# Rotary attention into a mixture of experts on one core: plan products and gathers one slot earlier, a dense step one tile later, four casts on another engine

## The chip, the cores and the metric

The kernel runs on one core of a Trainium2 chip. The metric is the device time of one execution in microseconds (us). A core has five engines that run their own instruction streams and wait for each other through semaphores: TensorE (PE in the profile, its weight loads PEld), VectorE (DVE), ScalarE (ACT), GpSimd (POOL) and SyncE (SP), which here only issues transfers. Data moves between the chip's main memory and the core's SBUF by DMA; matmul results land in PSUM.

## What is computed

The reference is attention with rotary position coding, followed by a layer of one dense network and eight experts. Shapes: batch 8, 8 heads, 576 positions, head size 64; the layer sees 4608 tokens of width 512, and all its hidden widths are 512.

```python
q_rot, k_rot = (rotate(q), rotate(k))
scores = scale * np.matmul(q_rot, k_rot.transpose(0, 1, 3, 2))
attn = softmax(scores)                      # row maximum subtracted
attn_out = np.matmul(attn, v)
x = attn_out.transpose(0, 2, 1, 3).reshape(B * S, H * D)

y_dense = np.maximum(x @ w1_dense, 0.0) @ w2_dense
logits = x @ w_gate
expert_idx = np.argmax(logits, axis=1)      # one expert per token
y_moe[mask] = gate_w[mask, None] * (np.maximum(x[mask] @ w1[e], 0.0) @ w2[e])
return y_dense + y_moe
```

## The kernel before

**Attention.** Heads are taken two at a time, so there are 32 pairs, four to a batch; `attention()` walks them with `for i in range(NP + 1)` and, inside, nine slots `t`. In slot `t` of pair `i` TensorE computes one block of scores of pair `i + 2` (`s1_block`, L369) whose row maximum VectorE takes (L371), one strip of transposed scores of pair `i` (`s2_strip`, L392) that ScalarE exponentiates into `pm` (L409), and some products with the values for pair `i - 1` (`av_part`, L431), which VectorE scales (`av_scale`, L442 to L445). The order on each engine is the order in which the Python code writes it: the schedule is written by hand, with tables that say which extra step goes to which slot `(i, t)`.

The rotary coding of pair `i + 5` runs on GpSimd as four long element-wise instructions (`stage_rope`, L314 to L317), after which a DMA transposes the result (L327) and another copies the keys to their own buffer (`stage_keys`, L355).

**The values.** The values of a batch arrive in float32 in one buffer `vf`. `cast_v(b, u)` (L273) turns the 128 columns of pair `u` of batch `b` into float16, 640 elements per partition in five groups; `v_turn` (L281, L282) transposes them on TensorE for the gate's weights. The casts of batch 0 stand ahead of the loop (pairs 0 and 1) and in slots 3 and 5 of pair 0 (pairs 2 and 3); those of batch 1 in slots 1 and 6 of pair 2 and later.

**The plan of tokens.** Tokens are sorted by expert into tiles of 128 rows. For the first six batches that plan is made while attention still runs: its steps sit in the table `steps[i, t]`. Its closing products (`e`, L633) are two runs of 15 matmuls of one-hot rows on TensorE into one PSUM tile; `f` (L638 to L653) turns the sum into row numbers on VectorE. `draw(0, u)` then gathers the rows of tile `u` of the first group (`gather`, L852, an indirect DMA that GpSimd issues, from the stored attention output `xd`) and has SyncE transpose it by DMA (`turn`, L858). For every tile but the first, ScalarE copies one column of row numbers ahead of the gather (L869).

**The experts.** `run_groups` walks the tiles `t` in groups of four. Per tile: the expert's first product (`expert_in`, L906) and its activation (L909); the transposition of that (`expert_turn`, L914); one to two of the four dense first products of the group (`dense_in`, L897, activation L899), which read the transposed tiles of the whole group at once; and the out tile of an earlier tile (`out_tile`, L921 and L923), whose rows VectorE copies (L925) and GpSimd scatters to the output (L926). How many dense products go to tile `t` is the tuple that the diff changes. A group's dense products are put on the list one tile ahead of the group's first tile.

Of the kernel before, what the change touches and what calls it, by code (L numbers as in the profile page):

```python
# [25 lines left out]
def kernel(  # L26
# [12 lines left out]
    nc = tc.nc  # L39
    B, H, S, D = q.shape  # L40
# [22 lines left out]
    VB = 2  # L63
    VC = D + 2 + 2 * E
    OA, VA, OB, WB = 2 * E, 2 * E + 2, D, D + 2
    v16s = []
    for i in range(VB):
        t = const_p.tile([P, HP, 5, 2 * VC], fp16, name=f"v16_{i}")
# [6 lines left out]
    with tc.tile_pool(name="setup", bufs=1) as setup_p:  # L75
# [37 lines left out]
        for b0, b1 in ((0, 5), (5, 9)):  # L113
            n = b1 - b0
# [14 lines left out]
    for i in range(NAT):  # L129
        t = early.tile([P, 9, 2, D], bf16, name=f"nat{i}")  # L130
# [139 lines left out]
                              v[b, a::2, MAIN:S, :].rearrange("h p d -> p h d"))  # L270

    def cast_v(b, u):
        nc.scalar.copy(v16s[b % VB][:, u, :, VA:VA + 2 * D].rearrange("p n (h d) -> p n h d", d=D),  # L273
                       vf[:, u].rearrange("p (h n) d -> p n h d", n=5))

    def v_turn(b, u):
        if u == 0:
# [393 lines left out]
    def attention():  # L671
        for f in turn_early(0):
            f()
        stage_keys(1, nc.sync)
        for part in range(2):
            stage_load(1, 0, 2, part, (0, HP))
        split_gate()
        for i in range(1, KK):
            pad_keys(i)
        for t in range(9):  # L680
            s1_block(0, t)
        for t in range(9):
            s1_block(1, t)
            if t == 1:
                shift_rows(0)
                for part in range(2):
                    stage_load(1, 2, 4, part, ())
                nc.scalar.copy(ident_h, ident_f)
                nc.scalar.preload_act_table_set("natural_log_exp_and_others")
                cast_v(0, 0)  # L690
            if t == 2:
                early_2 = turn_early(2)
            if 3 <= t < 7:
                early_2[t - 3]()
        cast_v(0, 1)
        for i in range(3, RA):
            stage_rope(i)
        stage_transpose(3)
        gt = gate_steps(0, wg)
        rk, got0 = rank_steps(0, wg, attn_sums)  # L700
        WS = [(i, 5) for i in range(5, 22, HP)] + [(24, 5), (25, 1), (25, 6), (26, 1), (26, 6)]
        assert len(WS) == E + 2
        steps = {(27, 0): gt[0:1], (22, 0): [route_first, route_ranks, route_tokens], (27, 2): gt[1:2], (27, 4): gt[2:3]}
        AVS = (((0, 0), (0, 1), (1, 3), (3, 4), (4, 5), (5, 7), (7, 8), (8, 9), (9, 10)),
               ((0, 0), (0, 1), (1, 3), (3, 4), (4, 5), (5, 6), (6, 7), (7, 8), (8, 10)))
        loads = {}
        for b in range(2, B):
            n = (b - 2) * HP
            for at, f, *x in ((n, stage_load, b, 0, 2, 0, ()), (n + 1, stage_load, b, 0, 2, 1, ()),
                              (n + 1, stage_tails, b, 0), (n + (1 if b in (2, B - 1) else 2), stage_tails, b, 1),  # L710
                              (n + 2, stage_load, b, 2, 4, 0, ()), (n + 3, stage_load, b, 2, 4, 1, ())):
                loads.setdefault(at + (1 if b == 2 else 0), []).append((f, *x))
        V0 = (0, 2), (0, 7), (1, 3), (1, 5)
        v_steps = {}
        for b in range(1, B):
            n = b * HP
            for u, (c, r) in enumerate((((n - 3, 6), (n - 3, 8)), ((n - 2, 3), (n - 2, 5)), ((n - 1, 3), (n - 1, 5)), ((n, 2), (n, 5)))):
                if b == B - 1 and u > 1:
                    c = (n - 1, 1 + 3 * (u - 2))
                if b == 1 and u < 2:  # L720
                    c, r = ((n - 2, 1), (n - 2, 5)) if u == 0 else ((n - 2, 6), (n - 2, 8))
                v_steps.setdefault(c, []).append((cast_v, b, u))
                v_steps.setdefault(r, []).append((v_turn, b, u))
        for i in range(NP + 1):
            for t in range(9):
                if i + 2 < NP:
                    s1_block(i + 2, t)
                if i < NP:
                    s2_strip(i, t)
                if 1 <= i <= NP and t >= 1:  # L730
                    for k in range(*AVS[i % HP == 1][t]):
                        av_part(i - 1, k)
                    if t == 8:
                        av_scale(i - 1)
                if i == 0 and t in (3, 5):
                    cast_v(0, 2 + t // 5)
                if (i, t) in V0:
                    v_turn(0, V0.index((i, t)))
                if i < NP and (i, t) in v_steps:
                    for f, *x in v_steps.pop((i, t)):  # L740
                        f(*x)
                if t == 1 and i + 1 < NP:
                    shift_rows(i + 1)
                if t == 2 and i + RA < NP:
                    stage_rope(i + RA)
                if t == (0 if i > 1 else 2) and i + KA < NP:
                    stage_keys(i + KA, nc.sync)
                if t == 2 and i + LA < NP:
                    stage_transpose(i + LA)
                if t == 2:  # L750
                    for f, *x in loads.pop(i, ()):
                        f(*x)
                if (i, t) in WS:
                    n = WS.index((i, t))
                    load_w(*((w1d, moe_w1_dense), (w2d, moe_w2_dense))[n] if n < 2 else (w1e[:, n - 2], moe_w1[n - 2]))
                if t == 5:

                    if i % HP == 0 and i // HP + 1 < B:
                        stage_v(i // HP + 1)
                    if i % HP == 3 and HP < i < NP - HP or i == NP - 3:  # L760
                        x_store(i // HP - 1)
                    if i == NP - RA:
                        early_cm.__exit__(None, None, None)
                        open_late()
                        wa = late["wa"]
                        pl, mm, fin = plan_steps(0, wa, attn_sums, got0)
                        w2 = [lambda e=e: load_w(late["w2e"][:, e], moe_w2[e]) for e in range(E)]
                        steps[27, 6] = rk[0:1] + [route_parts]
                        steps[27, 5] = w2[0:2]
                        steps[27, 7] = w2[2:5]  # L770
                        steps[28, 0] = rk[1:2] + w2[5:6] + pl[0:1]
                        steps[28, 2] = gt[3:4]
                        steps[28, 3] = rk[2:3] + w2[6:8] + pl[1:2]
                        steps[28, 6] = rk[3:4]
                        steps[29, 0] = pl[2:3]
                        steps[29, 3] = pl[4:6]
                        steps[29, 8] = rk[4:5]
                        steps[30, 0] = rk[5:6]
                        steps[30, 6] = mm[0:1]
                        steps[30, 7] = mm[1:] + [fin, lambda: draw(0, 0)]  # L780
                        for n in range(1, GT):
                            steps[31, 3 * n - 2] = [lambda n=n: draw(0, n)]
                        steps[31, 8] = pl[3:4]
                if (i, t) == (NP - 1, 2):
                    logit_sum(B - 2)
                for st in steps.pop((i, t), ()):
                    st()
            if i < NP:
                s2_tails(i, 0)
            if i < NP:  # L790
                s2_tails(i, 1)
            if i in (0, 1) or i < NP and i % HP == 0:
                u0, u1 = (2 * i, 2 * i + 2) if i < 2 else (0, HP)
                for u in range(u0, u1, 2):
                    v_gate(u)
                v_part(i // HP, 0, u0, u1)
                steps.setdefault((i + 1, 0), []).append(lambda b=i // HP, u0=u0, u1=u1: v_part(b, 1, u0, u1))
            if i == NP - 1:
                draw(1, 0)
        assert not steps and not v_steps and not loads  # L800
        logit_sum(B - 1)
        x_store(B - 1, nc.scalar)
# [18 lines left out]
    GT = 4  # L821
# [42 lines left out]
    def draw(g, u):  # L864
        t = g * GT + u
        if u == 0:
            room(g, late["first"], g, 1)
        if t:
            nc.scalar.copy(take_i[:, t:t + 1], tk[:, t:t + 1])  # L869
        gather(g, u)  # L870
        if g == 0:
            turn(g, u)
# [80 lines left out]
    def run_groups(gs, plan):  # L953
# [23 lines left out]
        for g in gs:  # L977
            n = sizes[g]
            for u in range(n):
# [18 lines left out]
                    turns.append(ahead.pop(0))  # L998
                if t + 1 in starts:
                    dense += dense_steps(starts[t + 1])  # L1000
                m = len(dense) if t == last else (0, 1, 1, 2, 0, 1, 2, 2)[t] if t < 2 * GT else 1
                for st in dense[:m]:
                    st()
                del dense[:m]
# [49 lines left out]
```

## Time and profile before

| | us |
|---|---|
| median of 3 runs (460.21 to 466.31) | 464.79 |
| the profiled execution | 464.98 |
| its span, from the first to the last instruction | 463.2 |
| TensorE busy | 402.8 |
| GpSimd busy | 342.2 |
| VectorE busy | 320.9 |
| ScalarE busy | 295.8 |

The profile is of one execution; the runs around it differ by up to 6 us. Rows of a timeline give the start in us, the busy time, engine, source line and operation, what is written and read, and in brackets how long the engine stood idle before the row and what it seems to have waited for. Rows of the chain that ended last give start, duration, engine, tile and line. A row with `x4` holds four instructions that follow each other. Mean granted TensorE clock over the span: 0.972 of full speed.

### The profile page before, as it was taken

Reading aid. Unit: us, or ns where it says so; the run is one execution under the profiler, and the core shown is the slowest. Engines: PE = TensorE matmul, PEld = TensorE weight load, DVE = VectorE, ACT = ScalarE, POOL = GpSimd, SP = SyncE. Lnnn points to the kernel's source line nnn. Section 1 sums busy time; section 2 is a strip of 40 time slices with the busy share of each in tenths; the row PEclk is TensorE's granted clock in tenths of the full one; section 3 lists DMA queues with packets and bytes.
Section 4 is the critical chain, followed back from the end, with each engine's and each line's share of the span. In section 5 each row is a group of like instructions: output and inputs, shape, how many; then the busy total and the mean of one; then the engine's idle time right before and its main releaser. Section 6 shows DMA issues by size and latency. Waiting matters only on the chain.

```text
span 463.2 us, 11065 instructions
## 1 busy us (share of the span) xinstructions
PE 402.8 (87%) x4091; PEld 250.0 (54%) x4108; DVE 320.9 (69%) x579; ACT 295.8 (64%) x577; POOL 342.2 (74%) x279
## 2 busy tenths in 40 slices
PE   1688898989999999999988988786989999999991
PEld 0346566656666666666666665563435444444440
DVE  7887789888899999899999899964357211212221
ACT  6598787877887887887877886683333343333320
POOL 1799989989989979989999957933546455554332
PEclk9799899998999999999999998998999999999997
DMA  6866668988768868879968989928777777787442
GB/s 173 230 173 156 137 141 232 155 157 249 152 148 243 178 164 241 155 126 279 165 176 192 177 159 219 228 53 186 164 161 172 171 189 194 184 186 196 107 120 76
DMA packets 134251, 80.65 MB, mean 174 GB/s; under 512 B 93461, under 2 KB 127765, under 8 KB 134197
## 3 DMA queue, kind: packets, MB, share of 16 engines
q1 hardware_dynamic: 119460, 55.34, 52.0%
q0 software_dynamic: 14240, 23.73, 23.9%
q10 hardware_dynamic: 496, 0.85, 0.5%
q8 instruction: 35, 0.57, 0.5%
q14 instruction: 20, 0.16, 0.1%
HBM read 52.05 MB, written 14.42 MB: 144 GB/s over the span
## 4 chain that ended last, share of the span: by engine, by line
PE 64%; DMA 11%; ACT 9%; DVE 9%; issue 3%; SPq 2%; POOL 0%; POOLq 0%; ACTq 0%; DVEq 0%
PE s L369 10%; PE s L392 9%; PE av L431 9%; PE pd L897 7%; PE py L923 7%; PE py L921 7%; PE pe L906 7%; ACT pm L409 5%; DVE negm L371 5%; DMA qT<-mT 4%; PE vps L281 2%; PE s L365 2%; PE s L389 2%; DMA vf<-in_v_dram 2%; PE mps L377 2%
## 5 line engine op out<-in xcount | busy, mean ns | idle before, releaser
L371 DVE TENSOR_REDUCE negm<-s 128x1 f32<-128x576 f32 x288 | 205.3, 749 | 21.8 <-PE s L369 20.6
L409 ACT ACTIVATE pm<-s 128x512 f16<-128x512 f32 x280 | 161.5, 598 | 43.1 <-PE s L392 39.2
L431 PEld LDWEIGHTS <-pm 128*128 128x128 f16 x1600 | 87.3, 98 | 53.8 <-issue 21.6
L369 PE MATMUL s<-kx,qT 126*128 126x288 bf16 x512 | 108.0, 294 | 8.3 <-DVE negm L371 4.7
L392 PE MATMUL s<-qT,kx 128*128 128x64 bf16 (+1 forms) x502 | 107.0, 287 | 8.1 <-ACT pm L409 4.7
L431 PE MATMUL av<-v,pm 128*128 128x82 f16 x1600 | 100.6, 201 | 1.0 <-DVE v L300 0.5
L314 POOL TENSOR_TENSOR ra<-qk,cosx 128x1152 bf16<-128x1152 f32 x30 | 78.9, 2630 | 21.7 <-DVE nat L317 11.0
L925 DVE COPY y<-py 128x512 f32<-128x512 f32 x37 | 25.6, 691 | 90.2 <-PE py L923 89.1
L926 POOL DMA_INDIRECT out_dram<-y,put_i x37 | 37.4, 1012 | 54.2 <-DVE y L925 43.0
L909 ACT ACTIVATE hn<-pe,gp 128x512 bf16<-128x512 f32 x37 | 25.4, 687 | 75.4 <-PE pe L906 71.7
L317 POOL TENSOR_TENSOR nat<-ra,rb 128x1152 bf16<-128x1152 bf16 x30 | 70.9, 2363 | 2.4
L852 POOL DMA_INDIRECT xg<-xd,take_i x37 | 36.6, 989 | 26.2 <-ACT take_i L996 9.3
L369 PEld LDWEIGHTS <-qT 126*128 126x128 bf16 x512 | 40.4, 100 | 21.9 <-issue 13.3
L897 PE MATMUL pd<-xs,w1d 128*128 128x512 bf16 (+1 forms) x160 | 38.9, 369 | 4.3 <-DMA xs<-xg 2.0
L315 POOL TENSOR_TENSOR rb<-qk,sinx 128x576 bf16<-128x576 f32 x30 | 42.1, 1404 | 0.0
L316 POOL TENSOR_TENSOR rb<-qk,sinx 128x576 bf16<-128x576 f32 x30 | 42.1, 1404 | 0.0
L392 PEld LDWEIGHTS <-kx 128*128 128x128 bf16 x512 | 35.2, 97 | 12.1 <-issue 3.1
L906 PE MATMUL pe<-w1e,xs 128*128 x144 | 38.3, 386 | 2.0 <-DMA xg<-xd,take_i 0.8
L923 PE MATMUL py<-w2e,he 128*128 x146 | 37.7, 379 | 0.4 <-issue 0.2
L921 PE MATMUL py<-w2d,hd 128*128 128x512 bf16 x141 | 37.3, 379 | 0.3
L899 ACT ACTIVATE hd<-pd 128x512 bf16<-128x512 f32 (+1 forms) x40 | 22.5, 565 | 10.0 <-PE pd L897 6.2
L897 PEld LDWEIGHTS <-w1d 128*128 128x128 bf16 x160 | 15.3, 99 | 23.0 <-issue 4.0
(178 smaller groups left out, 437.7 us busy)
## 6 DMA issues: line engine op xcount, KB each, us to landing
vf<-in_v_dram SPq DMA_DIRECT2D x8, 1024.0 KB
qk<-in_q_dram SPq DMA_DIRECT2D x15, 512.0 KB
qk<-in_k_dram SPq DMA_DIRECT2D x15, 512.0 KB
kx<-qT SPq DMA_DIRECT2D x30, 144.0 KB
w1e<-in_moe_w_dram POOLq DMA_DIRECT2D x8, 512.0 KB, 6.8
w2e<-in_moe_w_dram POOLq DMA_DIRECT2D x8, 512.0 KB, 13.0
xd<-xn SPq DMA_DIRECT2D x7, 512.0 KB
vf<-in_v_dram SPq DMA_DIRECT2D x16, 64.0 KB
```

What stands on the lines that cost most here:

```text
L314: eng.tensor_tensor(a, x, cx, AL.mult)
L315: eng.tensor_tensor(s[:, :, :, 0:half], x[:, :, :, half:D], sx[:, :, :, 0:half], AL.mult)
L317: eng.tensor_tensor(nat.rearrange("p c w d -> p w c d"), a, s, AL.add)
L369: nc.tensor.matmul(ps[:, c, 0:CH], lhsT=qT[:, t * P:(t + 1) * P], rhs=kT[:, k0 + c * CH:k0 + (c + 1) * CH], start=True, stop=True)
L371: nc.vector.tensor_reduce(state["negm", i][:, t:t + 1], ps[:, :, 0:CH], axis=AX.XY, op=AL.max, negate=True)
L392: nc.tensor.matmul(out_ap, lhsT=kT[:, s * P:(s + 1) * P], rhs=qT[:, qa if s < 4 else qb], start=True, stop=True)
L409: nc.scalar.activation(state["pm", i][:, ORDER.index(s), 0:MAIN], ps, AF.Exp, scale=float(scale))
L431: nc.tensor.matmul(state["av"][:, h, x * VC:(x + 1) * VC], lhsT=state["pm", i][:, 4 * h + n if n < 4 else 8, q0:q0 + P], rhs=v16s[b % VB][ ...
L897: nc.tensor.matmul(ps[:, 0:n], lhsT=w1d[:, dt, ft * P:(ft + 1) * P], rhs=xs[:, 0:n, dt, :], start=(dt == 0), stop=(dt == DT - 1))
L906: nc.tensor.matmul(ps, lhsT=xs[:, u, dt, :], rhs=w[:, 0, dt, :], start=(dt == 0), stop=(dt == DT - 1))
L921: nc.tensor.matmul(py, lhsT=hd[:, ft, u], rhs=w2d[:, ft, :], start=(ft == 0), stop=False)
L923: nc.tensor.matmul(py, lhsT=he[:, ft], rhs=w[:, 0, ft, :], start=False, stop=(ft == FT - 1))
```

## The change

There are three parts. In the table of steps, the first run of the plan's closing products goes from slot 6 of pair 30 to slot 5, the second run with `f` and the first gather from slot 7 to slot 6, and the gathers of tiles 1, 2 and 3 from slots 1, 4 and 7 of pair 31 to slots 0, 2 and 4. In the experts' loop, tile 7 issues one dense product in place of two and tile 8 two in place of one. Four of the 32 casts of values are issued on VectorE in place of ScalarE: pairs 2 and 3 of batch 0 and pairs 0 and 1 of batch 1.

```diff
     def cast_v(b, u):
-        nc.scalar.copy(v16s[b % VB][:, u, :, VA:VA + 2 * D].rearrange("p n (h d) -> p n h d", d=D),
-                       vf[:, u].rearrange("p (h n) d -> p n h d", n=5))
+        f = nc.vector.tensor_copy if (b, u) in ((0, 2), (0, 3), (1, 0), (1, 1)) else nc.scalar.copy
+        f(v16s[b % VB][:, u, :, VA:VA + 2 * D].rearrange("p n (h d) -> p n h d", d=D),
+          vf[:, u].rearrange("p (h n) d -> p n h d", n=5))
...
-                        steps[30, 6] = mm[0:1]
-                        steps[30, 7] = mm[1:] + [fin, lambda: draw(0, 0)]
+                        steps[30, 5] = mm[0:1]
+                        steps[30, 6] = mm[1:] + [fin, lambda: draw(0, 0)]
                         for n in range(1, GT):
-                            steps[31, 3 * n - 2] = [lambda n=n: draw(0, n)]
+                            steps[31, 2 * n - 2] = [lambda n=n: draw(0, n)]
...
-                m = len(dense) if t == last else (0, 1, 1, 2, 0, 1, 2, 2)[t] if t < 2 * GT else 1
+                m = len(dense) if t == last else (0, 1, 1, 2, 0, 1, 2, 1, 2)[t] if t <= 2 * GT else 1
```

On each engine the change moves the following. TensorE: the first 15 products go ahead of two strips and five value products, the last 15 ahead of five value products; four dense matmuls go behind an out tile. ScalarE: three copies of row numbers go ahead of one to three exponentials each, four casts are gone. VectorE: four casts more, each behind a row maximum. The order on GpSimd and SyncE is the same.

## The prediction

> **What bounds the kernel now.** I read the page first, then the busy time by stretches, then the timeline of each engine around the places that the diff touches, and beside it the chain that ended last.
>
> ```profile
> span 463.2 us, 11065 instructions
> ...
> PE 64%; DMA 11%; ACT 9%; DVE 9%; issue 3%; SPq 2%; POOL 0%; POOLq 0%; ACTq 0%; DVEq 0%
> ```
> ```profile
> 20.00:60.00 40.00, 33.61 (x346) 21.49 (x347) 30.71 (x50) 31.01 (x60) 39.14 (x23) 0.90 0.70 165
> ...
> 300.00:340.00 40.00, 33.96 (x310) 18.95 (x314) 21.67 (x59) 20.95 (x50) 18.11 (x18) 0.96 0.64 144
> ...
> 380.00:420.00 40.00, 39.79 (x183) 18.10 (x186) 7.97 (x12) 15.41 (x24) 23.02 (x24) 1.00 0.78 188
> ```
>
> The columns of the stretches are the busy us of PE, PEld, DVE, ACT and POOL, then the granted clock. TensorE carries most of the chain. It is full from 380 us on (39.79 of 40), where the chain ends; the open time lies at the start (33.61 of 40) and where attention hands over to the experts (33.96). What shortens TensorE's path in those two stretches comes through to the end. Every part of the change lies in one of the two.
>
> The hand-over, TensorE's timeline first, then the chain of DMA work that it waited for:
>
> ```profile
> 315.72 1.02 PE L906 MATMUL pe<-w1e,xs 128*128 x3 [0.83 <-DMA xg<-xd,take_i]
> 317.36 1.02 PE L906 MATMUL pe<-w1e,xs 128*128 x4 [0.62 <-DMA xs<-xg]
> 320.36 1.05 PE L897 MATMUL pd<-xs,w1d 128*128 128x512 bf16 x4 [1.98 <-DMA xs<-xg]
> ```
> ```profile
> 309.33 4.79 DMA xg<-xd,take_i
> ...
> 314.14 1.19 SPq L858
> ...
> 316.73 3.50 DMA xs<-xg
> ```
>
> The first dense product needs all four transposed tiles of the first group. The fourth landed at 320.22 (316.73 + 3.50), and TensorE stood 0.62 + 1.98 = 2.60 us for tiles two to four. The 0.83 before the first I take for its own sequencer, which reads the expert's number there; it stays.
>
> **Part 1, products and gathers a slot sooner.** The instructions are the same; 30 small products (two runs of 15) move ahead of two strips, and the ACT copies of indices with their gathers move up. From the chain and the timelines:
>
> ```profile
> 304.84 0.54 PE sums L633 x15
> 305.38 0.18 PE av L431 x5
> ```
> ```profile
> 306.14 0.24 DVE L638 COPY p<-sums 128x80 f32<-128x80 f32 x1 [1.82 <-PE sums L633]
> ...
> 307.63 1.10 POOL L852 DMA_INDIRECT xg<-xd,take_i  x1 [6.26 <-ACT pm L416]
> 309.33 0.98 POOL L852 DMA_INDIRECT xg<-xd,take_i  x1 [0.61 <-ACT take_i L869]
> 310.88 0.95 POOL L852 DMA_INDIRECT xg<-xd,take_i  x1 [0.57 <-ACT take_i L869]
> ...
> 327.98 0.95 POOL L852 DMA_INDIRECT xg<-xd,take_i  x1 [0.30 <-issue]
> ```
>
> In the new order the second run of 15 passes only one run of five value products (0.18), so the plan ends about 0.18 sooner, not a whole slot: the strips that the first run passes were TensorE's work of that slot, and they are still to be done. They go 0.54 later; the strip behind them stays where it was, and ACT, which reads them, has idle time in between. If it had none, the price is 0.54. The first gather starts near 307.45. The second then waits for POOL alone: 1.10 of the first and the 0.30 between gathers that follow each other, so 308.85 (0.48 sooner); by the same spacing the third near 310.1 (0.78 sooner) and the fourth near 311.4. The fifth keeps its place, and POOL, SP and VectorE keep their order here.
>
> What this is worth hangs on one landing.
>
> ```profile
> DMA to landing us min/median/max: 2.9/3.0/4.8
> ```
> ```profile
> q0 software_dynamic: 46, 0.13, 37.1%
> ```
> ```profile
> q1 hardware_dynamic: 415, 0.11, 115.7%
> ```
>
> The first row is all gathers from 300 to 335 us; the second is the gathers' DMA queue from 310.6 to 311.8, the third the transposes' queue in the 0.6 us behind that. The second gather had moved 46 packets in its stretch (a gather is 48) when the first transposition came, and landed only when that was through: after 4.79 us in place of 2.9. From the first gather's start to that moment passed some 4.1 us; the second needed 1.70 (its later start) + some 2.5 = 4.2, and just missed. With starts 1.40 apart it needs 3.9 and makes it. Then the second transposition issues at about 311.8, not 314.14. The third and fourth follow their own gathers: with landings of 2.9 the last issues at 314.4 in place of 316.73 (gain 2.3), with 4.8 at 316.2 (gain 0.5). I take 1.5. Ends: 0.35 (the second gather misses again; everything shifts by the first one's 0.18 and a little) and 2.6 (all that TensorE stood).
>
> Behind that stand lies a second price.
>
> ```profile
> 318.00:321.40 3.40, 1.42 (x7) 0.55 (x6) 0.48 (x2) 0.77 (x2) 1.89 (x2) 0.98 0.89 213
> 321.40:324.80 3.40, 3.40 (x10) 1.18 (x8) 0.64 (x3) 1.52 (x4) 0.61 (x1) 0.52 0.64 139
> ```
>
> After 3.4 us with TensorE 1.42 busy, the granted clock was 0.52 for 3.4 us: 0.48 x 3.4 = 1.63 us lost. If the dense products start 1.5 sooner, the first stretch is 2.9 busy. I take half, 0.82, since the stretch over which activity counts may lie otherwise; ends 0 and 1.63. [...]
>
> **Part 2, third group's dense products one tile later.**
>
> ```profile
> 338.40 0.86 PE py L921 x4
> ```
> ```profile
> 343.65 1.02 PE L897 MATMUL pd<-xs,w1d 128*128 128x512 bf16 x4 [1.79 <-issue]
> ...
> 341.89 0.60 ACT L899 ACTIVATE hd<-pd 128x512 bf16<-128x512 f32 x1
> ...
> 336.85 2.52 SPq L858 DMA_TRANSPOSE xs<-xg  x2
> ```
>
> Four matmuls move, none is added. The product at 343.65 is the third group's first; no engine released it, and in the code it needs that group's four transposes, of which the last two were issued from 336.85. TensorE stood 1.79 us. In the new order the next out tile (8 matmuls, 2 x 0.86) and the next expert (0.86) come first, 2.6 of work that needs only older tiles; the out tile's fourth matmul needs the activation that ends at 342.49, about when TensorE gets there. So the product is reached at about 344.5, 0.85 after its data. Gain 1.75. If the transposes come later as well, less; ends 0 and 1.79. The two products that then stand in one tile take the two buffers that ACT empties in 0.60 each, while the out tile behind them runs 1.7.
>
> **Part 3, four casts on VectorE.**
>
> ```profile
> 55.62 0.61 ACT v L273
> ```
> ```profile
> 47.66 0.41 PE L369 MATMUL s<-kx,qT 126*128 126x288 bf16 x2 [0.89 <-DMA kx<-qT]
> ...
> 56.78 0.44 PE L281 MATMUL vps<-ident_h,v 128*128 128x128 f16 x5 [0.40 <-ACT pm L409]
> ```
> ```profile
> 29.70 4.37 DVE L371 TENSOR_REDUCE negm<-s 128x1 f32<-128x576 f32 x6
> ...
> 54.62 2.15 DVE L371 TENSOR_REDUCE negm<-s 128x1 f32<-128x576 f32 x3 [0.35 <-PE s L369]
> ...
> 57.68 0.31 DVE L445 TENSOR_TENSOR lw<-av,rz 128x160 f32<-128x160 f32 x1
> ```
> ```profile
> 30.00 2.63 POOL L314 TENSOR_TENSOR ra<-qk,cosx 128x1152 bf16<-128x1152 f32 x1
> 32.59 1.40 POOL L315 TENSOR_TENSOR rb<-qk,sinx 128x576 bf16<-128x576 f32 x1
> ...
> 280.99 0.69 POOL L545 TENSOR_TENSOR run<-run,hs 128x240 f32<-128x240 f32 x1 [1.07 <-DVE ni L515]
> ```
> ```profile
> 281.01 0.69 DVE L516 TENSOR_SCALAR nf<-ni 128x8 f32<-128x8 f32 x1
> ...
> 334.93 0.17 DVE L516 TENSOR_SCALAR qf<-rf 128x10 f32<-128x10 f32 x1
> ```
> ```profile
> L115 DVE COPY cosx<-sc 128x320 f32<-128x320 f32 x1 | 0.5, 486 | 0.5 <-ACT sc L111 0.5
> ```
>
> ACT loses four times some 0.61 us. The two of pair 0 are worth nothing at the end: pair 2 starts at 47.66 on a DMA of keys for which TensorE already waits 0.89. Of the two in pair 2 the later one (55.62) is on the chain, and behind it TensorE waits 0.40: gain 0.4.
>
> VectorE gains four operations that the trace does not show there. The nearest row for the work is L115, 320 elements in five groups in 0.486; a cast has 640, so under twice that, 0.8. The nearest row for a wait is L516: eight elements took 0.69 us beside a POOL instruction that ran over the same time, ten took 0.17 elsewhere. So VectorE was held until POOL was done, and in the first pairs POOL is busy 39.14 of 40 us with rope instructions of 1.4 to 2.6. The first cast stands behind the second of the six reductions from 29.70, at about 31.2, inside the instruction from 30.00 to 32.63: held 1.4. Read the same way, the others are held 0 to 1.4, 1.3 and 1.1. Behind each wait the row maxima, which free TensorE's score buffers. In pair 0 that is about 2 us on VectorE, less the stand of 0.89: some 0.8 at pair 2, about as much as POOL's own wait for VectorE puts on the keys. In pair 2 the last cast, behind the first reduction from 54.62, ends near 58.0, so the value transpose that TensorE issues at 56.78 waits for it, and the weights' sums at 57.68 end near 60.6, which holds pair 3's value products: another 0.9, less the 0.4. Sum +1.3. Ends: -0.4 (not held) and +3.
>
> [...]
>
> **The sum**, against the profiled execution's own 464.98 us (span 463.2 and 1.78 around it; the runs' median is 464.79, from 460.21 to 466.31): 464.98 - 1.5 - 0.82 - 1.75 + 1.3 = 462.2 us.
>
> **Rivals.** (a) The second gather is caught by the transposition again. For it: the margin is 0.2 us. Against: POOL spaces the gathers evenly. Then 0.35 and no clock gain: 464.2. (b) The casts are not held. [...] Against: L516. 462.2 - 1.7 = 460.5. (c) Slower: a held cast loses to POOL's next instruction too, since these stand back to back. One more, 2 us in the mean, for each of four casts is 8 on VectorE; if 2 of it lie under TensorE's slack, that adds 6: 468.2. It decides when part 3 costs over 4.1, what the rest gains. Against it: L516 got in at the first end. (d) Part 2 doesn't do what it says, because the third group's transposes come later by as much as the product: 462.2 + 1.75 = 463.9.
>
> **How the numbers follow.** Forecast 0.40, (a) 0.27, (b) 0.18, (c) 0.09, (d) 0.06. The low end takes every gain at its end: 464.98 - 2.6 - 1.63 - 1.79 - 0.4 = 458.6. The high end has the small gather gain, part 2 whole and the casts at +3: 464.98 - 0.35 - 1.75 + 3 = 465.9. Only (c) lies outside. Two per cent, about what a measurement of this kernel can tell from no change, is 9.3 us; no case gets there, so faster 0.03, same 0.94, slower 0.03.
>
> **What would show it.** Right: a second gather that lands in about 3 us, under 1 us of waiting at the first dense product, none before the third group's first product, casts on VectorE of 1 to 2 us. Wrong: casts of 0.4 to 0.8 us beside busy POOL, a second gather of over 4 us, a wait as long as before at the third group, or a pair 3 that starts over 2 us later.

## The result and the profile after

The changed kernel took 468.89 us (median of five executions, 467.56 to 471.94) against 464.79: a ratio of 1.0121, 95% interval 1.0074 to 1.0167. I had forecast 462.2 with a range up to 465.9, so the change went the other way. The profiled execution, the fastest of the five, took 467.56, 2.58 more than that of before, with a span of 465.8. In three later measurements, of twelve executions each, the same kernel came to 1.0023, 1.0032 and 1.0006; most of the loss first measured did not come back. The first ratio stays under the two per cent below which the forecast had called a time the same. In all ratios of this document, executions over 1.5% above the fastest of their kernel are left out.

The page's head and the answer by stretches (PE, PEld, DVE, ACT, POOL busy, then granted clock):

```profile
span 465.8 us, 11083 instructions
```
```profile
20.00:60.00 40.00, 32.55 (x317) 20.39 (x317) 32.67 (x48) 26.82 (x50) 39.14 (x23) 0.91 0.66 154
300.00:340.00 40.00, 33.52 (x333) 20.55 (x332) 21.09 (x57) 21.14 (x51) 18.14 (x17) 0.91 0.66 145
380.00:420.00 40.00, 40.00 (x187) 18.11 (x185) 7.60 (x11) 15.41 (x24) 23.13 (x24) 1.00 0.79 184
37.40:44.20 6.80, 6.12 (x60) 4.02 (x59) 3.71 (x7) 3.45 (x8) 6.64 (x5) 0.52 0.67 168
316.90:323.70 6.80, 5.32 (x56) 4.20 (x56) 3.41 (x10) 1.94 (x6) 0.94 (x1) 0.50 0.34 74
```

TensorE still ends the chain and is full from 380 us on. In the first stretch it is busy 32.55 in place of 33.61; in the hand-over the mean clock fell from 0.96 to 0.91. Two stretches of 6.8 us ran at half clock, one right behind the first two casts, one in the hand-over.

The casts beside GpSimd (timeline of VectorE and GpSimd):

```profile
30.47 2.63 POOL L315 TENSOR_TENSOR ra<-qk,cosx 128x1152 bf16<-128x1152 f32 x1
32.54 0.97 DVE L274 CAST v<-vf 128x640 f16<-128x640 f32 x1
33.05 1.58 POOL L316 TENSOR_TENSOR rb<-qk,sinx 128x576 bf16<-128x576 f32 x1
34.60 1.40 POOL L317 TENSOR_TENSOR rb<-qk,sinx 128x576 bf16<-128x576 f32 x1
34.76 1.66 DVE L274 CAST v<-vf 128x640 f16<-128x640 f32 x1
51.85 2.36 POOL L318 TENSOR_TENSOR nat<-ra,rb 128x1152 bf16<-128x1152 bf16 x1
52.70 1.93 DVE L274 CAST v<-vf 128x640 f16<-128x640 f32 x1
58.31 1.41 POOL L317 TENSOR_TENSOR rb<-qk,sinx 128x576 bf16<-128x576 f32 x1
58.55 1.58 DVE L274 CAST v<-vf 128x640 f16<-128x640 f32 x1
```

Each cast ends 0.41 or 0.42 us after the GpSimd instruction that ran when it began: 33.10 and 33.51, 36.00 and 36.42, 54.21 and 54.63, 59.72 and 60.13. Later traces bear this out: of the 36 casts on VectorE in nine traces, this one among them, 35 end 0.41 or 0.42 behind that GpSimd instruction, and one 0.51. So a cast's own work is read as 0.41, and the rest as waiting. It gets in at the first end, and the GpSimd instruction at 33.05 took 1.58 where its like takes 1.40. What TensorE then waited for:

```profile
34.22 0.41 PE L370 MATMUL s<-kx,qT 126*128 126x288 bf16 x2 [0.88 <-DVE negm L372]
37.13 0.64 PE L370 MATMUL s<-kx,qT 126*128 126x288 bf16 x2 [1.16 <-DVE negm L372]
54.87 0.38 PE L393 MATMUL s<-qT,kx 128*128 128x512 bf16 x1 [0.83 <-DVE mT L381]
60.19 0.45 PE L282 MATMUL vps<-ident_h,v 128*128 128x128 f16 x5 [0.55 <-DVE v L274]
```

The hand-over in the same timeline:

```profile
310.49 1.10 POOL L853 DMA_INDIRECT xg<-xd,take_i  x1 [5.99 <-ACT pm L417]
311.89 0.98 POOL L853 DMA_INDIRECT xg<-xd,take_i  x1 [0.30 <-ACT take_i L870]
313.17 0.95 POOL L853 DMA_INDIRECT xg<-xd,take_i  x1 [0.30 <-issue]
314.43 0.95 POOL L853 DMA_INDIRECT xg<-xd,take_i  x1 [0.31 <-issue]
...
316.58 1.08 ACT L410 ACTIVATE pm<-s2w 128x512 f16<-128x512 f32 x2 [1.93 <-PE s L393]
316.80 0.22 DVE L443 RECIPROCAL rz<-av 128x10 f32<-128x10 f32 x1 [4.68 <-remote]
318.21 0.21 PE L390 MATMUL s<-qT,kx 128*64 128x64 bf16 x1 [2.96 <-ACT pm L410]
...
322.18 2.67 PE L907 MATMUL pe<-w1e,xs 128*128 x8 [0.17 <-issue]
324.68 0.59 PE L898 MATMUL pd<-xs,w1d 128*128 128x512 bf16 x2
...
331.34 0.60 ACT L900 ACTIVATE hd<-pd 128x512 bf16<-128x512 f32 x1 [1.55 <-PE pd L898]
332.00 0.39 PE L922 MATMUL py<-w2d,hd 128*128 128x512 bf16 x1 [1.33 <-issue]
347.05 0.39 PE L922 MATMUL py<-w2d,hd 128*128 128x512 bf16 x1 [0.39 <-ACT hd L900]
348.51 1.02 PE L907 MATMUL pe<-w1e,xs 128*128 x4 [0.21 <-issue]
349.37 0.81 PE L898 MATMUL pd<-xs,w1d 128*128 128x512 bf16 x3
```

The gathers follow each other by 1.40, 1.28 and 1.26 as I had read them, the first dense product starts without a wait, and so does the third group's at 349.37. But in pair 31 ACT, VectorE and TensorE stood: ACT began an exponential 1.93 us late, VectorE the reciprocal, and TensorE waited 2.96 for ACT. I call this the stand; I had not foreseen it. At 331.34 ACT began late again, by 1.55 us, and the first out tile on TensorE waited 1.33.

By marks, the span's 2.6 us more splits so (to rounding; a mark is ACT's first copy of `mT` in a pair; +1.33 stands ahead of pair 1, where the change has no part): pairs 1 to 4 +2.10 (30.66 to 32.76); pair 4 to 31 -0.37; pair 31 to the first expert product +3.41 (14.30 to 17.71); from there to the first dense product -2.14; the rest of TensorE's work -1.32; the end -0.34.

### The profile page after: what moved, and what is told of

Same layout as the page of the kernel before. It is cut to its first block, busy times and chain, and to the rows that moved or that the text cites. A ratio compares the mean times of both kernels' runs of the same rounds, so it can differ in the third digit from the quotient of the medians.

```text
span 465.8 us, 11083 instructions
## 1 busy us (share of the span) xinstructions
PE 406.4 (87%) x4108; PEld 252.0 (54%) x4108; DVE 326.1 (70%) x583; ACT 293.7 (63%) x573; POOL 342.9 (74%) x279
## 5 line engine op out<-in xcount | busy, mean ns | idle before, releaser
L370 PE MATMUL s<-kx,qT 126*128 126x288 bf16 x512 | 109.1, 296 | 9.9 <-DVE negm L372 7.3
L922 PE MATMUL py<-w2d,hd 128*128 128x512 bf16 x148 | 38.3, 379 | 1.7 <-issue 1.3
L898 PE MATMUL pd<-xs,w1d 128*128 128x512 bf16 (+1 forms) x160 | 37.8, 363 | 0.5 <-issue 0.5
L390 PE MATMUL s<-qT,kx 128*64 128x512 bf16 x64 | 18.3, 286 | 11.7 <-ACT pm L410 8.6
```

The costliest lines, as they stand in the source:

```text
L370: nc.tensor.matmul(ps[:, c, 0:CH], lhsT=qT[:, t * P:(t + 1) * P], rhs=kT[:, k0 + c * CH:k0 + (c + 1) * CH], start=True, stop=True)
L898: nc.tensor.matmul(ps[:, 0:n], lhsT=w1d[:, dt, ft * P:(ft + 1) * P], rhs=xs[:, 0:n, dt, :], start=(dt == 0), stop=(dt == DT - 1))
L922: nc.tensor.matmul(py, lhsT=hd[:, ft, u], rhs=w2d[:, ft, :], start=(ft == 0), stop=False)
```

## The experiments

Each was timed in twelve executions beside the kernel before, which ran 35 times beside each set of four (22 times beside e17 and e18). Medians are those of all executions. Four chips were used: one for e1 to e4, one for e5 to e8, one for e9 to e12, and one for e13 to e18.

**The parts alone.** e1:

```
-        nc.scalar.copy(v16s[b % VB][...], vf[:, u]...)
+        f = nc.vector.tensor_copy if (b, u) in ((0, 2), (0, 3), (1, 0), (1, 1)) else nc.scalar.copy
+        f(v16s[b % VB][...], vf[:, u]...)
```

> Only part 3: the four casts of values on VectorE, everything else as before. Theory C (the casts are the loss, about 3.5 us where I had summed 1.3): 3 to 4 us over the kernel before, a ratio near 1.0075, with the casts at 0.97 to 1.93 us and pair 3 some 3 us later, as in the changed kernel. Rival G (the earlier gathers are the loss, by the stand of TensorE, ACT and VectorE in pair 31): 1 to 1.5 us over, a ratio near 1.003.

1.0017, interval 0.9978 to 1.0055; medians 465.46 and 463.79, a ratio of 1.0036. Three of the twelve took 469.57 to 472.05; the slowest of 35 executions of the kernel before took 467.38. That is rival G's 1.003 within the interval, and theory C's 1.0075 is outside it. The trace is used below.

e2:

```
-                        steps[30, 6] = mm[0:1]
-                        steps[30, 7] = mm[1:] + [fin, lambda: draw(0, 0)]
+                        steps[30, 5] = mm[0:1]
+                        steps[30, 6] = mm[1:] + [fin, lambda: draw(0, 0)]
...
-                            steps[31, 3 * n - 2] = [lambda n=n: draw(0, n)]
+                            steps[31, 2 * n - 2] = [lambda n=n: draw(0, n)]
```

> Only part 1: the plan's closing products and the first group's gathers a slot sooner. Theory C: 1 to 2.5 us under the kernel before (0.995 to 0.998), the first dense product without a wait, and no stand of ACT and VectorE in pair 31. Rival G: 0 to 3 us over (1.000 to 1.006), and between 314 and 318 us a stand of about 2 us in which ACT and VectorE begin work whose inputs have long been there, as in the changed kernel.

0.9934 (0.9898 to 0.9969), 461.99 us, no stand. Part 1 gains by itself, 3.1 us by the ratio and 1.4 at the interval's near end; rival G falls for part 1 alone. The first dense product still waited, for 2.16 us, where theory C had no wait.

e3:

```
-                m = ... (0, 1, 1, 2, 0, 1, 2, 2)[t] if t < 2 * GT else 1
+                m = ... (0, 1, 1, 2, 0, 1, 2, 1, 2)[t] if t <= 2 * GT else 1
```

> Only part 2: the third group's dense products one tile later. If the wait of 1.79 us is filled as I read it: 1.2 to 1.8 us under the kernel before (0.996 to 0.9975), with under 0.7 us of waits at the moved products. Rival: the four transposes come later by as much, and the ratio is 1.000.

0.9991 (0.9959 to 1.0023). No gain that can be told from nothing; the forecast of 1.2 to 1.8 us (0.996 to 0.9975) lies in the lower part of the interval, so the time alone does not exclude it.

e4 is parts 1 and 2, e2 with e3:

> Parts 1 and 2 without the casts. Theory C (each part's effect adds up; the casts are the whole loss): 2.5 to 4 us under the kernel before (0.991 to 0.995). Rival G: about as before or slower (0.998 to 1.004), as the gathers lose what the dense products gain.

0.9917 (0.9884 to 0.9950), 460.67 us. So the loss comes with the casts. But e1 to e3 add up to 0.994, and the whole had 1.012.

**Do the parts act on each other?** e5 is the changed kernel; e6 and e7 are it without part 2 and without part 1.

> The whole change once more, on the same chip as its parts. The parts alone measured 1.0017 (casts), 0.9934 (plan and gathers) and 0.9991 (dense), which add up to 0.994; the whole had measured 1.012. Theory S (the parts add up, and the first measurement of the whole caught unlucky executions): 0.993 to 0.999. Theory I (the parts act on each other): again 1.007 to 1.017, and the stand of TensorE, ACT and VectorE at 314.7 to 316.6 us is there again.

> Parts 3 and 1: the casts with the earlier products and gathers, third group's dense products as before. Theory S: 0.993 to 0.999. Theory I, if it is casts against gathers (VectorE's and ACT's instructions shifted by four, just where the gathers come earlier): 1.006 to 1.017, with the stand in pair 31.

> Parts 3 and 2: the casts with the later dense products, products and gathers as before. Theory S: 0.998 to 1.003. Theory I, if it is casts against gathers: also 0.998 to 1.003, and only e6 and the whole are slow; if it is casts against dense products: 1.006 to 1.017 here.

e5 1.0023 (0.9989 to 1.0057; medians 465.39 and 463.98), e6 1.0073 (1.0037 to 1.0109), e7 1.0037 (0.9996 to 1.0078; median 468.13, with seven of its twelve executions between 467.46 and 470.45). Neither sum nor the first measurement. In e5 and e6 the stand was there; the first expert product came 16.65 and 17.60 us behind pair 31's mark.

e8 is the changed kernel with the casts on VectorE written in another form:

```
...
+            nc.vector.tensor_reduce(dst, src[:, :, :, :, None], axis=AX.X, op=AL.max)
...
```

> The whole change, with the four casts on VectorE written as a maximum over an innermost axis of one element, which writes the same values. [...] Rival: VectorE is slow beside busy GpSimd in whatever form: 1.0 to 1.9 us each, and the time of e5.

I had expected casts of 0.65 to 0.85 us in this form, and 1 to 3 us under e5. 1.0068 (1.0028 to 1.0108), not under e5: in time a miss. The stand was here too (17.59 behind the mark). On the casts the lines decide. The source line's group in e8, then in e5 (duration in ns, minimum, median, maximum):

```profile
L276 DVE TENSOR_REDUCE v<-vf x4: 807/808/810, 32.5 to 54.8; 128x640 f16<-128x640 f32 x4
```
```profile
L274 DVE CAST v<-vf x4: 695/1237/1649, 32.5 to 55.8; 128x640 f16<-128x640 f32 x4
```

The same work took 0.807 to 0.810 beside a GpSimd that was as busy (39.14 of the 40 us from 20 us on, as in the changed kernel's first trace), at half the rate of the 0.41 read above and in none of the four longer by a wait. That VectorE is slow beside GpSimd in whatever form is refuted. So in this pair the copy has 0.41 of own work and a wait, the reduction 0.81 and no wait; what makes the one wait and the other not, no run shows.

**Is the stand due to ACT's program?** In the four traces with the stand, part 1 was in and ACT had four instructions fewer. The trace shows packets of two instruction queues (on the changed kernel's page 35 packets of some 16 KB and 19 of some 8 KB), which I took for blocks in which the programs arrive; four instructions fewer could put the end of a block into pair 31. This is theory F. e9 gives ACT its count back:

```
...
+            nc.vector.tensor_copy(dst, src)
+            for _ in range(2 if (b, u) == (0, 2) else 1):
+                nc.scalar.copy(ap.tile([P, 5, 2, 2], fp16, tag="tiny", bufs=1, name="tiny"), src[:, :, :, 0:2])
...
```

> The whole change, with five ACT copies of 20 elements (0.2 us each) where four casts left ACT's program, so that from pair 3 on each ACT instruction has the number that it has without the casts. Theory F (ACT's instructions are fetched in blocks; four fewer of them put the end of a block into pair 31, beside the earlier gathers, and ACT stands there): the stand between 8.7 and 12.1 us behind pair 31's row-maximum turn is gone, first expert product 14.2 to 14.5 us behind it in place of 16.7 to 17.7, and the time 2 to 4 us under the whole change; what is left over e12 is the hold of the casts, 1.5 to 3 us. Rival R (it is the casts on VectorE, whatever ACT's count): the stand stays, and so does the time (1.002 to 1.010).

e10 does it with e8's reduction:

> As e9, with the casts in the form that is not held (0.81 us each). Theory F: no stand in pair 31, 1.5 to 3 us under e9, and about the time of e12 (0.988 to 0.995). Rival R: the stand stays, 1.003 to 1.010, as e8.

e11 leaves the casts on ACT and gives VectorE four tiny reductions; e12 is e4 again.

> Parts 1 and 2 with all casts on ACT, and four VectorE operations of 20 elements (some 0.1 us each) at the places of the four casts: VectorE's program is as long as in the whole change, ACT's as long as before. Theory F for ACT: no stand in pair 31 and the time of e12. Rival V (VectorE's block ends where it hurts, not ACT's): the stand is there, and 2 to 4 us over e12.

> Parts 1 and 2 alone once more (the kernel of e4), as the comparison for the three others on the same chip: 0.988 to 0.995 by both theories, no stand in pair 31.

e9 1.0006 (0.9967 to 1.0046), e10 0.9971 (0.9931 to 1.0010), e11 0.9970 (0.9933 to 1.0006), e12 0.9950 (0.9917 to 0.9982). No stand in any: 14.2 to 14.3 us behind the mark. In e9 and e10 that is what theory F wanted, but e11 and e12, which have no stand by that theory either, ran on the same chip, so the chip could be the reason. The times fit in part: e10 is 1.6 us under e9, as forecast, but some 1 us over e12. Next, theory F's own condition was tested without casts, e13 (parts 1 and 2) taking four ACT instructions from the set-up, e14 the same without part 1, with e15 (the changed kernel) and e16 (the kernel of e9):

```
-        nc.scalar.activation(edge[:, 0:1], sc[:, 1, 0, 0:1], AF.Copy, scale=0.0)
-        nc.scalar.activation(edge[:, 1:2], edge[:, 0:1], AF.Identity, bias=ends)
+        nc.vector.memset(edge[:, 0:1], 0.0)
+        nc.vector.tensor_copy(edge[:, 1:2], ends)
...
-            nc.scalar.copy(vf[r, :, n, :], edge[r, 0:1, None].broadcast_to([D, HP, D]))
+            nc.vector.memset(vf[r, :, n, :], 0.0)
```

> Parts 1 and 2 with all casts on ACT, and four other small ACT instructions of the set-up (two for edge, two for the padding of vf) on VectorE: ACT's program is as short as in the whole change, with no cast on VectorE. Theory F (ACT's count together with the earlier gathers makes the stand in pair 31): ACT's stand is there, first expert product 16.6 to 17.8 us behind pair 31's row-maximum turn, and 1.5 to 4 us over parts 1 and 2 alone, so 0.998 to 1.004. Rival R (something else of the casts): no stand, 14.2 to 14.5, and 0.991 to 0.996.

> Part 2 alone with the same four ACT instructions gone, products and gathers as before. Theory F with both conditions: no stand, first expert product 14.2 to 15.6 us behind, and the time of part 2 alone (0.996 to 1.002). If ACT's count alone brings the stand: 16.6 to 17.8 and 1.002 to 1.008.

> The whole change, as the comparison for e16 on the same chip: 1.002 to 1.012, first expert product 16.6 to 17.8 us behind.

> The kernel of e9 (whole change, ACT's count restored with five copies of 20 elements) beside the whole change on one chip. Theory F: 1 to 3 us under e15, first expert product 14.2 to 14.5 us behind. If the stand is made up for further on: the time of e15 within 0.5 us.

e13 0.9964 (0.9939 to 0.9989), e14 1.0032 (1.0006 to 1.0058), e15 1.0032 (0.9999 to 1.0065), e16 0.9999 (0.9971 to 1.0027). None has the stand, not even e15, which is the changed kernel; e13 is as rival R had it. e14's ratio is above the 1.002 that theory F allowed without a stand, though 1.002 lies in its interval; e13, which differs from it by part 1 alone, is 3.1 us faster. e16 is 1.5 us under e15, as theory F forecast, but e15 has no stand that could be the reason. The timeline of e15 in the place of the lines shown above:

```profile
313.39 1.12 ACT L410 ACTIVATE pm<-s2w 128x512 f16<-128x512 f32 x2
...
315.05 0.19 PE L390 MATMUL s<-qT,kx 128*64 128x64 bf16 x1 [0.82 <-ACT pm L410]
...
317.96 1.02 PE L907 MATMUL pe<-w1e,xs 128*128 x4 [0.74 <-DMA xg<-xd,take_i]
...
321.98 1.02 PE L898 MATMUL pd<-xs,w1d 128*128 128x512 bf16 x4 [1.68 <-DMA xs<-xg]
```

Theory F falls in the form in which I held it: the same program stands in some executions and not in others. Nor do the packets tell them apart: in all twenty traces one of the 16 KB packets starts 9.6 to 10.8 us behind pair 31's mark, and no other instruction packet starts between 8.7 and 12.1, where the stand is. A last pair on one chip, the changed kernel and parts 1 and 2 alone:

> The whole change once more, beside parts 1 and 2 alone on one chip. The stand in pair 31 was in the first profile of the whole change and in all three with casts and earlier gathers on chip 9 (e5, e6, e8), but not in e15 on chip 11. Theory F (ACT's count and the earlier gathers, in some executions): it can be here and not in e18. Rival H (the chip or the hour, not the program): here and in e18 alike, or in neither. The time by either: 1.5 to 6 us over e18, since the casts cost that much on each chip so far.

> Parts 1 and 2 alone, beside e17: 0.990 to 0.996, first expert product 14.2 to 14.5 us behind pair 31's row-maximum turn by theory F. By rival H: the stand is here if it is in e17.

e17 1.0006 (0.9973 to 1.0038), medians 463.45 and 463.30; e18 0.9974 (0.9936 to 1.0011). The casts' 1.5 us over e18 is at the near end of the forecast, and e18 itself is above its 0.990 to 0.996. Two executions of e18 took 666 and 2131 us. No stand in either profile, so the pair does not tell a weaker theory F from rival H. Over all, seven traces have part 1 and ACT's shorter program: four with the stand, in the first measurement and on the chip of e5 to e8, and three without (e13, e15, e17), all on the last chip. In e18, whose gathers came through fast, the first dense product needed no wait at all:

```profile
315.43 1.02 PE L906 MATMUL pe<-w1e,xs 128*128 x4 [0.49 <-issue]
316.29 1.03 PE L897 MATMUL pd<-xs,w1d 128*128 128x512 bf16 x4
```

**The stages, read over all traces.** One profile is one execution, but twenty of them, before and after among them, allow means. Pairs 1 to 4 hold all four casts that the change moves; the time between ACT's marks of pairs 1 and 4, with what the clock lost in it (missing clock by time; half speed over one stretch of 3.41 us is 1.71):

| kernels | first cast, us | pair 1 to 4, us | clock lost, us |
|---|---|---|---|
| casts on ACT: e2, e3, e11, e18 | | 29.10 to 29.13 | 0 |
| casts on ACT: before, e4, e12, e13, e14 | | 30.39 to 30.71 | 1.71 |
| held: e5, e9 | 0.70, 0.83 | 29.76, 29.90 | 0 |
| held: e6 | 1.45 | 30.62 | 1.71 |
| held: after, e1, e7, e15, e16, e17 | 0.97 to 1.69 | 32.76 to 33.43 | 3.41 |
| reduction: e8, e10 | 0.81 | 28.45, 28.46 | 0 |

At full clock the four held casts together cost 0.7 over ACT's, and the four reductions save 0.65. The larger price is the clock: the mean of the nine held traces is 32.0, that of the nine with casts on ACT 29.9. Seven of the nine held traces, all with a first cast of 0.97 or more, take 12.3 to 12.6 us from pair 1 to 2, with half clock in it; the casts on ACT take 10.0 to 10.3 there. In marks (the changed kernel, then e5):

```profile
30.54 0.24 ACT L380 CAST mT<-mps 9x128 bf16<-9x128 f32 x1
42.83 0.25 ACT L380 CAST mT<-mps 9x128 bf16<-9x128 f32 x1
```
```profile
30.47 0.24 ACT L380 CAST mT<-mps 9x128 bf16<-9x128 f32 x1
41.29 0.24 ACT L380 CAST mT<-mps 9x128 bf16<-9x128 f32 x1
```

12.29 against 10.82, the casts in e5 being shorter. So the half clock goes with the longer first cast in all nine; what in it brings it was not tested. In the seven, TensorE was busy 1.54 to 1.90 of the 3.41 us ahead of the half clock, but that is no sure sign: in e15 a stretch with 1.77 was followed by full clock, in e12 one with 2.19 by half.

In the hand-over, from pair 31's mark to the first dense product: 18.94 to 20.83, mean 19.8, in the five traces without part 1; 16.58 to 20.05, mean 18.45, in the eleven with part 1 and no stand; 18.77 to 20.35, mean 19.8, in the four with the stand. And from the first dense product to TensorE's last, less the clock lost in it: 129.53, 130.67 and 131.69 in three traces without part 2 (e1, e2, before), mean 130.6; 130.22 to 131.21, mean 130.56, in the thirteen with part 2 and no stand; 132.07 to 133.98, mean 133.2, in the four with the stand.

## Why the prediction was wrong

Two terms of the sum failed, and one thing was not in it. Part 2's gain of 1.75 was not there; the casts cost 2.1 where I had 1.3; and the stand, in the executions that have it, costs some 3.6. The range was too narrow for the first of these: its high end, 465.9, still counted part 2's gain whole, and would have been 467.6 without it.

**The casts: mechanism right, size too small.** They are held by GpSimd, as I read from the row of L516, and rivals (b) and (c) are both out: all but two of the 36 took over 0.8 us (the two 0.55 and 0.70), and none was held by a second instruction. The waits appear where I put them, down to the value transpose at 60.19. The step that failed is the price, +1.3: in the stage they cost 2.1 in the mean of nine traces, some 0.7 of direct delay and 1.4 of lost clock. I had priced the clock behind TensorE's stand in the hand-over and not behind the stands that the casts make. Of the signs that I had named for a wrong forecast this one came: pair 3's mark is 2.2 us later (50.70 to 52.89), though 1.3 of it stood ahead of the casts. Timed on one chip the casts come to 0.8 us (e1), 2.6 (e9 over e12, with ACT's small copies) and 1.5 (e17 over e18), which alone would not tell 2.1 from 1.3.

**Part 1: right in its gain and its first step, not in all of its path.** The spacing of the gathers is as worked out. The second transposition, which I had moved up to 311.8, or 10.4 us behind pair 31's mark, starts 10.2 to 10.4 behind it in fourteen of the fifteen traces with part 1 (12.7 in before, 11.5 in e10). The gathers' time to landing, least, median and most, in before was 2.9, 3.0 and 4.8; in e17:

```profile
DMA to landing us min/median/max: 2.9/3.0/3.5
```

The second gather gets through in time here; in e2 one still took 4.6. But the sign that I named, under 1 us of waiting at the first dense product, came in only one of the eleven traces with part 1 and no stand (e18, none); the others waited 1.42 to 3.41. Their fourth transposition starts 13.8 to 14.8 us behind the mark (15.3 in before), where gathers that all land in 2.9 would have given 13.0. And before's second gather had the worst of it: in the four other traces without part 1 the second transposition starts 10.8 to 11.8 behind the mark. So there is luck in the size: I took 1.5 of gain; the traces without the stand have 1.34 in the mean. The clock is better, too: all five traces without part 1 lost 1.7 us to half clock behind the first dense product, and of the eleven with it and no stand only three did (e9, e10, e16), which is 1.2 in the mean where I took 0.82. That little work ahead brings the half clock was my reading of two rows of before (1.42 of 3.40 us busy, then 0.52); as a rule no run shows it. Together 2.6, and I had 2.3. Timed, e2 gained 3.1, e13 3.1 over e14, and e4, e12 and e18 between 1.2 and 3.9, part 2 included.

**Part 2: wrong by its whole gain, as far as the traces tell.** The wait of 1.79 before the third group's product does go (in twelve of the thirteen traces with part 2 and no stand; 0.79 is left in e7), but it was not a cost of its own. Where the first dense product waits longer, the third group's wait is short or gone: 1.98 and 1.79 in before, 2.16 and 0.80 in e2, 2.90 and none in e1. That the one row of gathers and transposes which feeds both makes it so is my reading. I took the rest of one wait, as one execution showed it, for a gain: the remaining time is 130.6 without and 130.56 with. Only three traces stand for the first figure, and they spread over 2.2 us; timed, part 2 is worth 0.4 us in e3 and 0.8 from e2 to e4, neither apart from nothing. Rival (d) had the size, 463.9, but not the step: with transposes as late as the product the wait would have stayed.

**The stand: not in the sum at all.** It put the first expert product 2.4 to 3.5 us late in the changed kernel, e5, e6 and e8, and so took part 1's gain away (19.8 to the first dense product, as without part 1). And it was not over there: from the first dense product on, these four lose no clock and still take 133.2 in place of 130.56, in three of them with a second wait of 1.33 to 1.37 at the first out tile. From pair 31's mark to TensorE's last product they take 152.95 in the mean, the eleven traces with part 1 and no stand 149.35: 3.6 us. It was seen only with part 1 and the casts off ACT together, but not in e15 and e17, which have both; all later traces with it come from one chip. Whether the program takes part in it, and what makes it, stays open.

With the measured sizes, -2.5 for parts 1 and 2 together (the mean of e4, e12 and e18 is 0.9947) and +2.1 for the casts, 464.79 becomes 464.4, a ratio of 0.999; the three repeats say 1.0006 to 1.0032. The first measurement's median, 468.89, lies 3.5 to 5.4 us above the medians of those three. With the stand's 3.6 the sum would be 468.0, an estimate from the traces; but of the five executions only the profiled one is known to have had it, and e5, whose profile has it too, had a median of 465.39. So the first measurement's excess is explained in part at most. The version that beats both kernels is parts 1 and 2 without the casts: 0.9917, 0.9950 and 0.9974 in three measurements, the last not apart from 1.

## What to carry to other kernels

Before moving a copy to VectorE beside a busy GpSimd, look for short VectorE instructions that last as long as a GpSimd one (L516 in before: eight elements in 0.69 us, and ten in 0.17 elsewhere). Here 35 of 36 such copies ended 0.41 or 0.42 us behind the GpSimd instruction that ran when they began, and a form with twice the own work was the faster: 0.81 us against 0.97 to 1.93 for the changed kernel's casts. Price a new wait on TensorE with the clock that may fall behind it: from pair 1 to 4, six of the nine held traces lost 3.41 us of clock, those with the casts on ACT none or 1.71. And a wait far down a chain of transfers is not a gain to be taken: see whether the wait ahead of it grows when it shrinks.

## What the runs showed of the hardware

- A cast of 640 elements in five groups of 128 ended 0.41 or 0.42 us behind the GpSimd instruction that ran when it began, in 35 of 36 casts; written as a reduction it took 0.81, twice that, and did not wait (e8, e10). L115 in before, 0.486 us for 320 elements, did not foretell the 0.41.
- Executions of one program differ in which stretches of 3.41 us run at half clock: from 20 us on to pair 31, one in e18 (1.71 us lost) and some six in e4 (10.67), which are one and the same kernel. Executions of the kernel before ranged over 459.73 to 469.50 us.
- TensorE, ACT and VectorE can stand together for some 2 us in one execution and not in another of the same program (ACT 1.93 us late at 316.58 in the first trace and TensorE's wait for it 2.96; in e15's trace no wait of ACT is shown there, and 0.82 on TensorE).
